# Storing the last 64 rows of each batch two batches at a time, and adding the last item in two halves

## The chip, the core and the metric

The kernel runs on one core of one Trainium2 chip. The metric is the device time of one execution in microseconds. The three runs of the kernel before the change took 427.37, 427.93 and 429.17 us; their median, 427.93 us, is the time before.

## What is computed

Eight batches of eight heads of sparse attention (576 positions, head width 64) are followed by a spectral mixing layer and a residual layer. With `x` the attention output of shape (8, 576, 512):

```python
X = np.fft.rfft(x, axis=1)
Y[:, :n_modes] = Yr + 1j * Yi        # 64 modes, each with its own complex 512x512 matrix w_r, w_i
y = np.fft.irfft(Y, n=S, axis=1)
u = x + y
return u + np.maximum(u @ w_ch, 0.0)
```

The output is 8 x 576 x 512 in float32, 9.44 MB. A batch is 576 rows of 512 floats, 2 KB a row.

## The kernel before

**Up to the last stage.** The kernel computes strided and local attention, takes the Fourier coefficients of the result, and multiplies the 64 modes by their matrices while those are fetched. The matrices are fetched by `w_fetch` through the GpSimd queue, with conversion to half precision. A usual fetch (L186) has 64 partitions with two rows of 2048 numbers each. Three pairs of modes, named in `UNEVEN`, have the first of their two fetches cut into pieces (L182): of 25, 12 and 27 partitions, of 6, 54 and 4, and of 10 and 54.

**The last stage, from about 395 us.** The residual `u` and the product `u @ w_ch` are finished and stored item by item. The list `items` has 18 entries. The first 16 are a pair of batches and one of four blocks `t` of 128 rows of each. The last two, with `t == 4`, are the rows 512 to 575, of batches 0 to 3 (item 16) and of batches 4 to 7 (item 17, `LAST`). An item fills a tile `osb` of 128 partitions x 2 x 512 floats, 512 KB. For `t < 4` each of the two halves `osb[:, j]` is one batch. For `t == 4` the half `osb[:, i]` holds two batches: the first in partitions 0 to 63, the second in partitions 64 to 127.

**Steps of one item.** TensorE adds the inverse transform to two sums that are held in PSUM (`v_early`, `u_early`, `new_rows`). `v_done` (L1013) applies Relu on ScalarE. `u_done` (L1020) adds the two sums on VectorE into `osb` and issues the stores. The function `pieces` says in how many slices `v_done` and `u_done` work: two for item 0, one for all others.

**Stores.** For `t < 4` an item is stored from SyncE (L1028): one transfer with 128 partitions outermost and two rows of 2 KB in each, or, for item 0, two transfers of 256 KB. For `t == 4` the kernel before issues one transfer of 128 KB for each batch (L1031), even batches from SyncE and odd ones from ScalarE; each has 64 rows of 2 KB on both sides.

**Order.** The program order is the order on each engine. In round `k` of the last loop `v_done(k)` stands before `u_done(k - 1)`, so ScalarE applies the Relu of item 17 before it issues the stores of item 16. Nothing of the kernel follows `u_done(17)` but the end of the program (L1108 in the trace), which waits for the stores. `osb` shares its five buffers with the fetched matrices; no fetch is left in the last stage.

Of the kernel before, what the change touches and what calls it, by code (L numbers as in the profile page):

```python
# [56 lines left out]
def kernel(  # L57
# [10 lines left out]
    nc = tc.nc  # L68
# [169 lines left out]
    def normalise(val, den, n, pieces, dst):  # L238
        rec = pin.tile([128, 8], FP, tag="rec", bufs=4, name="rec")
        nc.vector.reciprocal(out=rec[0:n, 0:pieces], in_=den)  # L240
        nc.vector.tensor_tensor(  # L241
            out=dst,
            in0=val.rearrange("p h (q c) -> p h c q", c=4),
            in1=rec[0:n, 0:pieces]
            .to_broadcast((n, pieces, 64))
            .rearrange("p h (q c) -> p h c q", c=4),
            op=AluOp.mult,
        )
# [718 lines left out]
    for n, i in enumerate([3, 5, 7] + list(range(8, 21))):  # L967
        b, t = n // 2, n % 2 * 2
# [8 lines left out]
    LAST = len(items) - 1  # L977
# [25 lines left out]
            )  # L1003

    def pieces(k):
        return [slice(0, 1), slice(1, 2)] if k == 0 else [slice(0, 2)]

    def v_done(k):
        rl = ptr.tile([128, 2, 576], FP, tag=("xT", "rl")[k // 2 % 2], bufs=2, name="rl")
        rls[k] = rl[:, :, 0:DM]  # L1010
        vp = vps.pop(k)
        for j in pieces(k):
            nc.scalar.activation(out=rls[k][:, j], in_=vp[:, j], func=ACTF.Relu)  # L1013

    def u_done(k):
        bs, t = items[k]
        up, rl = ups.pop(k), rls.pop(k)
        osb = pw.tile([128, 2, DM], FP, tag="w", name="osb")
        for j in pieces(k):
            nc.vector.tensor_tensor(  # L1020
                out=osb[:, j], in0=up[:, j], in1=rl[:, j], op=AluOp.add
            )
            if t < 4:
                rows = out[:, ds(128 * (t - t % 2), 256), :].rearrange(
                    "b (p i) e -> p b i e", i=2
                )
                own_b = slice(bs[0] + j.start, bs[0] + j.stop)
                nc.sync.dma_start(rows[:, own_b, t % 2], osb[:, j])  # L1028
        if t == 4:
            for b in bs:  # L1030
                (nc.scalar if b % 2 else nc.sync).dma_start(  # L1031
                    out[b, ds(512, 64), :], osb[ds(64 * (b % 2), 64), b // 2 % 2, :]
                )

    flush()
# [24 lines left out]
    for k in range(2):  # L1060
        if k:
            u_early(k)
        new_rows(k, ups[k], yys)
        u_done(k)
    for k in range(2, LAST + 2):
        if k == 8:
            held = psum("p", pair=True)[:, 0]
            spec_z(3, 1, held)
            act_copy(zzs[1], held)
        if k <= LAST:  # L1070
            v_early(k)
        if k > 2:
            u_early(k - 1)
        if k <= LAST:
            new_rows(k, vps[k], zzs)
        if k > 2:
            new_rows(k - 1, ups[k - 1], yys)
        if k <= LAST:
            v_done(k)
        if k > 2:  # L1080
            u_done(k - 1)
# [31 lines left out]
```

## Time and profile before

| what | value |
|---|---|
| runs | 427.37, 427.93, 429.17 us; median 427.93 us |
| profiled execution | the page gives its span, 426.7 us, 1.2 us under the median of the runs |
| busy share of the span | PE 81%, VectorE 55%, ScalarE 51%, GpSimd 26% |
| output stores | 17 from L1028, 8 from L1031 |
| first store issued, last store issued | 396.88 us, 422.32 us |
| last store landed | 425.58 us |
| granted TensorE clock, mean | 0.926 |

Times are counted from the first instruction of the profiled execution. In the answers on the trace, a line of a timeline has its start, its duration, the engine, the source line, the operation, the output and input tiles, and in brackets the idle time before it and what ended it; `SPq` and `ACTq` are the instruction queues of SyncE and ScalarE, where stores are issued. In a table by stretches there stand the busy time of each engine with its instructions in brackets, then the granted clock, the mean busy share of the 16 DMA engines, and the rate in GB/s. In the list of DMA issues stand the tiles, the queue, the count, the size of each, and the median time in us from issue to landing.

### The profile page before, as it was taken

What the parts mean: (1) busy time and instruction counts of PE and PEld (TensorE: products, weight loads), DVE (VectorE), ACT (ScalarE), POOL (GpSimd) and SP (SyncE); (2) the same over time, 40 slices, a digit from 0 to 9 for tenths busy, and PEclk for the clock granted to TensorE, in tenths of its full rate; (3) what the DMA queues carried; (4) which work ended last, traced back from release to release, by engine and by line L of the source; (5) the groups of instructions that cost most, each with busy time, mean ns of one, the idle gap of its engine ahead of it and who ended that gap; (6) DMA issues with size and microseconds to landing.
All of it is one profiled execution on the core that took longest, in us unless ns stands there. A gap on an engine that the chain in (4) does not pass through costs nothing.

```text
span 426.7 us, 9768 instructions
## 1 busy us (share of the span) xinstructions
PE 346.4 (81%) x4167; PEld 208.2 (49%) x4167; DVE 234.7 (55%) x466; ACT 218.3 (51%) x390; POOL 110.7 (26%) x196
## 2 busy tenths in 40 slices
PE   2977878769999698889768788878788867889993
PEld 2866767554656365566433344435444423445330
DVE  3788778851355154356113246746676354655884
ACT  1687678643656356556642235423442444443872
POOL 8332333322423222222222322222232222210000
PEclk9999899967999689999995889989999979989997
DMA  8999999999999999999999999999999999995698
GB/s 150 210 212 212 213 213 213 211 211 211 214 213 213 213 213 215 212 214 215 210 214 211 213 214 213 210 213 215 212 213 214 213 213 214 214 212 105 244 355 287
DMA packets 30938, 91.62 MB, mean 215 GB/s; under 512 B 4464, under 2 KB 5232, under 8 KB 30896
## 3 DMA queue, kind: packets, MB, share of 16 engines
q0 software_dynamic: 25168, 81.28, 96.2%
q1 hardware_dynamic: 4976, 9.13, 5.9%
q10 hardware_dynamic: 752, 0.61, 0.5%
q8 instruction: 32, 0.52, 0.5%
q14 instruction: 10, 0.08, 0.0%
HBM read 162.83 MB, written 9.44 MB: 404 GB/s over the span
## 4 chain that ended last, share of the span: by engine, by line
DMA 47%; PE 29%; DVE 14%; ACT 5%; issue 3%; DVEq 0%; POOL 0%; ACTq 0%; POOLq 0%
DMA wt<-in_moe_w_i_dram 38%; DMA wt<-in_moe_w_r_dram 7%; PE y L597 5%; DVE xb L241 3%; DVE kz L283 3%; PE p L987 2%; ACT X L251 2%; PE sc L532 2%; PE tp L413 2%; PE sc L459 1%; PE p L1001 1%; PE y L532 1%; PE p L760 1%; DVE yy L752 1%; DVE rec L240 1%
## 5 line engine op out<-in xcount | busy, mean ns | idle before, releaser
L597 PE MATMUL y<-wt,X 128*32 128x512 f16 (+1 forms) x448 | 70.9, 430 | 20.1 <-DMA wt<-in_moe_w_i_dram 20.1
L186 POOL DMA_DIRECT2D wt<-in_moe_w_r_dram x59 | 34.7, 588 | 126.4 <-PE y L597 56.3
L186 POOL DMA_DIRECT2D wt<-in_moe_w_i_dram x60 | 35.4, 590 | 68.3 <-DMA wt<-in_moe_w_i_dram 44.4
L597 PEld LDWEIGHTS <-X 128*32 128x32 f16 (+1 forms) x448 | 28.1, 140 | 39.4 <-DMA wt<-in_moe_w_i_dram 18.6
L727 DVE COPY xo<-tp 128x512 f16<-128x512 f16 x32 | 22.1, 691 | 36.8 <-PE tp L725 36.8
L726 ACT ACTIVATE v<-sc 128x512 f16<-128x512 f32 x32 | 19.1, 597 | 44.2 <-PE sc L717 44.2
L717 PE MATMUL sc<-w_cp,xT 128*128 128x512 f16 x128 | 36.9, 410 | 1.9 <-DVE xT L690 1.9
L489 ACT ACTIVATE PL<-sc 128x480 f16<-128x480 f32 (+1 forms) x48 | 27.0, 578 | 21.3 <-PE sc L475 21.0
L241 DVE TENSOR_TENSOR xb<-av,rec 90x256 f16<-90x256 f32 (+2 forms) x80 | 36.0, 450 | 2.8
L240 DVE RECIPROCAL rec<-av 90x4 f32<-90x4 f32 (+2 forms) x80 | 14.6, 183 | 39.3 <-PE av L504 28.2
L251 ACT ACTIVATE yr<-y 128x512 f16<-128x512 f32 x28 | 16.7, 597 | 36.8 <-PE y L597 35.6
L961 DVE TENSOR_TENSOR xo<-p,xo 128x1024 f16<-128x1024 f32 x16 | 19.6, 1225 | 21.7 <-PE p L760 21.7
L420 DVE COPY qT<-tp 128x576 f16<-128x576 f16 x16 | 11.9, 752 | 34.7 <-PE tp L413 34.7
L251 ACT ACTIVATE v<-p 128x1024 f16<-128x1024 f32 x16 | 16.4, 1023 | 23.1 <-PE p L760 23.1
L378 ACT ACTIVATE PL<-sc 90x360 f16<-90x360 f32 (+1 forms) x48 | 22.7, 490 | 7.0 <-PE sc L371 6.4
L251 ACT ACTIVATE v<-tp 128x640 f16<-128x640 f16 (+1 forms) x24 | 19.0, 807 | 11.8 <-PE tp L447 9.3
L413 PE MATMUL tp<-cI_s,ring 64*64 64x64 f16 x864 | 22.4, 197 | 2.7 <-DVE qT L420 2.4
L459 PE MATMUL sc<-cMl_s,cI_s 128*128 128x480 f16 (+1 forms) x48 | 19.4, 405 | 4.5 <-ACT PL L489 2.9
L276 PE MATMUL tp<-cI_s,ring 72*128 72x72 f16 x256 | 15.4, 207 | 8.7 <-DMA ring<-in_v_dram 7.1
L413 PEld LDWEIGHTS <-ring 64*64 64x64 f16 x864 | 17.5, 110 | 9.4 <-issue 5.4
L251 ACT ACTIVATE kz<-tp 64x360 f16<-64x360 f16 (+1 forms) x32 | 18.9, 592 | 6.2 <-PE tp L413 5.2
L1013 ACT ACTIVATE rl<-p 128x1024 f32<-128x1024 f32 (+1 forms) x19 | 18.4, 979 | 5.7 <-PE p L1001 3.1
(142 smaller groups left out, 737.9 us busy)
## 6 DMA issues: line engine op xcount, KB each, us to landing
wt<-in_moe_w_i_dram POOLq DMA_DIRECT2D x60, 512.0 KB, 18.8
wt<-in_moe_w_r_dram POOLq DMA_DIRECT2D x59, 512.0 KB, 17.7
out_dram<-osb SPq DMA_DIRECT2D x15, 512.0 KB, 3.4
ring<-in_v_dram POOLq DMA_DIRECT2D x8, 288.0 KB, 13.4
ring<-in_q_dram POOLq DMA_DIRECT2D x8, 288.0 KB, 13.6
ring<-in_k_dram POOLq DMA_DIRECT2D x8, 288.0 KB, 13.1
ring<-in_v_dram POOLq DMA_DIRECT2D x3, 512.0 KB, 14.8
ring<-in_q_dram POOLq DMA_DIRECT2D x3, 512.0 KB, 14.8
```

What stands on the lines that cost most here:

```text
L186: nc.gpsimd.dma_start(dst, rows)
L241: nc.vector.tensor_tensor(out=dst, in0=val.rearrange("p h (q c) -> p h c q", c=4), in1=rec[0:n, 0:pieces] .to_broadcast((n, pieces, 64)) . ...
L251: nc.scalar.activation(out=out, in_=in_, func=ACTF.Copy)
L378: nc.scalar.activation(out=PS[0:n, ds(POFF[t], 4 * n)], in_=scp[0:n, 0 : 4 * n], func=ACTF.Exp, scale=SCALE,)
L413: nc.tensor.transpose(tp[ds(64 * hp, 64), ds(64 * i, 64)], qn[ds(64 * hp, 64), ds(64 * (9 * g + i), 64)], idn[ds(64 * hp, 64), ds(64 * hp, ...
L459: nc.tensor.matmul(scp[:, 0 : n * times].rearrange("p (h x) -> p h x", h=times), idn, mask_rows("cMl", n, times), start=True, stop=False,)
L489: nc.scalar.activation(out=dst, in_=src, func=ACTF.Exp, scale=SCALE)
L597: nc.tensor.matmul(yp[ds(a, 32), :], Xh[half][pr, c].rearrange("p b r (h m) -> p (b r h) m", h=2)[:, :, mm % 32], wt[pr, XC[c], :], start= ...
L717: nc.tensor.matmul(vp, xT[:, ch], w_chs["cp"][:, ch, :], start=(ch == 0), stop=(ch == 3),)
L726: nc.scalar.activation(out=v0, in_=vp, func=ACTF.Copy)
L727: nc.vector.tensor_copy(out=xo.rearrange("p (h q c) -> p h q c", h=2, c=4), in_=tp[:, 0:512].rearrange("p (h c q) -> p h q c", h=2, c=4),)
L961: nc.vector.tensor_tensor(out=xo, in0=up[:, 0:n], in1=xo, op=AluOp.add)
```

## The change

`pieces` gives two slices for the last item as well, so its Relu and its sum are each done in two instructions of 128 x 512 instead of one of 128 x 1024. The stores of the items 16 and 17 are issued in the loop over the slices, one transfer for each half of `osb` instead of one for each batch: source `osb[:, i]`, 128 partitions of 2 KB; destination two batches, 64 rows of 2 KB in each. The half 0 is stored from SyncE and the half 1 from ScalarE. For item 16, which has one slice, both are issued after its sum; for item 17 each is issued after its own half of the sum.

```diff
     def pieces(k):
-        return [slice(0, 1), slice(1, 2)] if k == 0 else [slice(0, 2)]
+        return [slice(0, 1), slice(1, 2)] if k in (0, LAST) else [slice(0, 2)]
...
                 nc.sync.dma_start(rows[:, own_b, t % 2], osb[:, j])
-        if t == 4:
-            for b in bs:
-                (nc.scalar if b % 2 else nc.sync).dma_start(
-                    out[b, ds(512, 64), :], osb[ds(64 * (b % 2), 64), b // 2 % 2, :]
+                continue
+            for i in range(2)[j]:
+                (nc.scalar if i else nc.sync).dma_start(
+                    out[ds(bs[2 * i], 2), ds(512, 64), :], osb[:, i]
                 )
```

## The prediction

> **What bounds the kernel now.** The change touches nothing before the last two of 18 items, so I read the page only for the span and then went to the end of the trace: the table by stretches, the list of store issues, the timeline of the last items. First the span, and the table by stretches; its last two columns are the busy share of the DMA engines and GB/s.
>
> ```profile
> span 426.7 us, 9768 instructions
> ```
> ```profile
> 410.00:418.00 8.00, 8.00 (x51) 2.56 (x50) 7.28 (x7) 6.33 (x7) 0.00 (x0) 1.00 1.01 376
> 420.00:421.00 1.00, 0.00 (x0) 0.00 (x0) 1.00 (x2) 0.00 (x0) 0.00 (x0) 1.00 1.03 393
> 421.00:422.00 1.00, 0.00 (x0) 0.00 (x0) 0.28 (x1) 0.00 (x0) 0.00 (x0) 0.96 0.94 244
> 422.00:425.00 3.00, 0.00 (x0) 0.00 (x0) 0.00 (x0) 0.00 (x0) 0.00 (x0) 0.50 0.88 307
> 425.00:426.70 1.70, 0.00 (x0) 0.00 (x0) 0.00 (x0) 0.00 (x0) 0.00 (x0) 0.50 0.00 0
> ```
>
> From 410 us on, all 16 DMA engines are full with stores; TensorE is full too until 418, but from 421.3 us no engine computes, and the DMA engines work on until 425. So the end is set by the stores: the last packet ends at 425.05 us by the trace's packet records, the last landing is at 425.58 (0.53 later), the span ends 1.1 after that. Whatever the stores of items 16 and 17 gain or lose arrives in the time in full.
>
> The timeline of the last two sums and the eight stores that the change replaces, and the list of store issues:
>
> ```profile
> 418.92 1.23 DVE L1020 TENSOR_TENSOR osb<-p,rl 128x1024 f32<-128x1024 f32 x1 [0.31 <-PE p L1001]
> 420.06 1.22 DVE L1020 TENSOR_TENSOR osb<-u,rl 128x1024 f32<-128x1024 f32 x1
> 420.17 2.44 SPq L1031 DMA_DIRECT2D out_dram<-osb  x4
> 420.18 2.75 ACTq L1031 DMA_DIRECT2D out_dram<-osb  x4
> ```
> ```profile
> out_dram<-osb SPq DMA_DIRECT2D x15, 512.0 KB, 3.4
> out_dram<-osb SPq DMA_DIRECT2D x2, 256.0 KB, 2.4
> out_dram<-osb SPq DMA_DIRECT2D x4, 128.0 KB, 2.8
> out_dram<-osb ACTq DMA_DIRECT2D x4, 128.0 KB, 3.3
> ```
>
> Four issues on each queue take 2.4 to 2.8 us, and the last goes out at 422.32, 1.0 us after the last sum ended. Every store is cut into packets of one row, 2 KB; a packet takes one DMA engine 84 to 85 ns (median), both at 397.5 us with one small store in flight and at 424.5 us with most engines idle. That is a price of the engine, not of the crowd.
>
> **What a transfer's outermost count does.** All 25 stores have 128 or 64 rows outermost, and each raises its semaphore at sixteen separate times, one for each DMA engine. The new destination has 2 batches outermost (64 rows inside), against 128 partitions in the source. No transfer of the SyncE and ScalarE queues in this trace has an outermost count under 64, so I looked for such transfers elsewhere, and found the cut fetches of L182 on the GpSimd queue. Issue times, then time to landing:
>
> ```profile
> 254.24 0.59 POOL L186 DMA_DIRECT2D wt<-in_moe_w_i_dram  x1 [1.62 <-DMA wt<-in_moe_w_i_dram]
> 257.07 0.59 POOL L182 DMA_DIRECT2D wt<-in_moe_w_r_dram  x1 [2.24 <-PE tp L685]
> 259.18 0.71 POOL L182 DMA_DIRECT2D wt<-in_moe_w_r_dram  x1 [1.52 <-DMA wt<-in_moe_w_i_dram]
> 261.62 0.61 POOL L182 DMA_DIRECT2D wt<-in_moe_w_r_dram  x1 [1.73 <-DMA wt<-in_moe_w_r_dram]
> ```
> ```profile
> wt<-in_moe_w_i_dram POOLq DMA_DIRECT2D x1, 512.0 KB, 19.5
> ...
> wt<-in_moe_w_r_dram POOLq DMA_DIRECT2D x1, 48.0 KB, 16.9
> ...
> wt<-in_moe_w_r_dram POOLq DMA_DIRECT2D x1, 432.0 KB, 19.0
> ...
> wt<-in_moe_w_r_dram POOLq DMA_DIRECT2D x1, 32.0 KB, 16.9
> ```
>
> The whole fetch of 64 partitions lands at 254.24 + 19.5 = 273.7 us; its three successors, of 6, 54 and 4 partitions and 512 KB in sum, at 274.0, 278.2 and 278.5: 4.8 us for what whole fetches land in 2.46 us. Between the first and the last of the sixteen semaphore marks of one fetch, whole fetches keep their distance for dozens in a row (6.1 to 6.4 us here); the fetch of 54 raises it from 6.28 to 9.90, and the one of 54 at 299.97 us brings it back from 9.11 to 5.58. A whole fetch is 128 packets, 8 for each engine, so a packet costs 2.46/8 = 0.307 us there. 3.6 us is 12 packets: 54 partitions x 2 rows = 108 packets lie on nine engines (12 each), and the other seven get none. Nine is the largest divisor of 54 that is not over 16. So on this queue the work is dealt out by the outermost count, in equal shares, and a count with no divisor near 16 leaves engines idle. For an outermost count of 2 that is two engines, 64 packets each.
>
> [...]
>
> **Part by part.** *Relu in halves:* two instructions of 0.594 us (the 128x512 rows of L1013) for one of 1.02, +0.17 us on ScalarE. The Relu of item 17 starts at 418.65 and would end at 419.84; VectorE is busy with item 16 until 420.15, which hides it; without that cover it costs 0.17. *Sum in halves:* two of 0.686 us for one of 1.22; from 420.06 the halves end at 420.75 and 421.43 instead of 421.28, +0.15 us for the second, −0.53 for the first. *Issues:* four instead of eight; SyncE at 420.17 and about 420.8, ScalarE at 420.18 and about 421.5 (the last 0.8 us earlier than now). ScalarE's stores stand behind the Relu of item 17, as before; behind them stands only the end of the program, on both queues. *Where the waiting goes:* to the DMA engines.
>
> *The new transfers.* They are 4 x 128 = 512 packets of 2 KB. The unknown is the number n of engines that share them. Its ends are 16 (the nearest stores, by size and source) and 2 (the nearest outermost count, by the rule the cut fetches show). I take 2: the two transfers differ from the stores of 256 KB at 397 us in nothing but the outermost count, and that is what the fetches react to. An engine's packet period in the full stretch is 16 x 2048 B / 377 GB/s = 87 ns. The engines come free of the store issued at 418.64 (landed 421.58 to 421.87, less the 0.53) at about 421.3. Then
>
> - n = 2: 512/2 = 256 packets x 0.087 = 22.3 us, last packet at 443.6, landing 444.1, span 445.2: +18.5 us.
>
> The second item's transfers queue behind the first's, which alone last 11 us, so their issue time costs nothing. The period has its own ends: 81 ns, the shortest packets (20.7 us, +17.0), and 94 ns, from 422 to 425 with both queues on an engine (16 x 0.88 x 2048 / 307; 24.1 us, +20.4). From 421.5 to 422.0 the packets, then almost all of one 64-partition half, took 162 ns in the median; two engines on different halves shouldn't meet that, and I keep it out of the range (41.5 us, +38).
>
> The median of the runs is 427.93, so I forecast 427.93 + 18.5 = 446.4 us. Against the 426.7 of the span this is the same 18.5.
>
> **The rivals.** *All 16 engines.* The destination's batches are dealt row by row. For it: nothing on these two queues shows another number than sixteen. Against it: the fetch of 54. Price: after 420.0 us the table has 393 + 244 + 334 + 326 + 260 (the stretch from 422 to 425 in single microseconds) = 1557 KB; at 380 GB/s, without the slow 64-row packets, they take 4.1 us and end at 424.1 instead of 425.05. That is at best −0.95, 427.0 us; if only the halves' delay shows, +0.15, 428.1. Either is within 0.5%, which is 2.1 us and about what a measurement of this kernel can tell from no change. The tail ends at 421.3 + 512 x 0.087/n, which meets the present 425.05 at n = 12: with 12 engines or more the change is not slower, at 8 it costs 1.8 us, so this rival decides the sign.
>
> *Two pairs of engines.* SyncE's and ScalarE's transfers go to different pairs: n = 4, 11.1 us, last packet at 432.4, +7.4, 435.3 us. For it: the trace doesn't say which engines a small count gets, and the distance between the first and last mark went up after one fetch of 54 and down after another, so there it was not always the same nine. Against it: that is the GpSimd queue; all sixteen engines serve SyncE's and ScalarE's stores alike now, and nothing in the trace keeps the two queues apart.
>
> **How the numbers follow.** Two engines 0.85, two pairs 0.04, sixteen 0.11. The likeliest case gives 446.4. Its range goes from +17.0 less the 0.6 by which the fastest run lies under the median and a microsecond for an earlier start (443.3), to +20.4 with the 1.2 by which the slowest lies over it and two for pauses between the queues (451.5); I leave a twentieth of the case outside, so it holds 0.81 and need not reach to the others. Slower by over 0.5%: 0.85 + 0.04 = 0.89; of the sixteen-engine case 0.10 within 0.5%, and 0.01 for a gain over 2.1 us, which no term here supplies.
>
> **What would show it.** Right: four stores at L1031 with 256 KB; DMA share near 0.125 and about 47 GB/s (2 x 2048/0.087) from 422 to 443; landings 11 us after the issue for item 16 and over 20 us for item 17; sums ending at about 420.75 and 421.4. Wrong: landings within 3.5 us and a span that ends near 426 (sixteen engines); 94 GB/s and 432 (two pairs); some 25 GB/s would be two engines with packets of 160 ns.

## The result: 446.36 us, 4.3% slower

The changed kernel takes 446.36 us in the median of four runs (445.82 to 446.80), against 427.90 us of the kernel before, the median of four runs (the three given above and one of 427.87 us). The ratio is 1.0429, with a 95% interval from 1.0416 to 1.0442. The profiled execution took 445.82 us; its span is 444.0 us, against 426.7.

**The profile after.** First the table by stretches of the changed kernel. Its last two columns are the busy share of the 16 DMA engines and the rate in GB/s.

```profile
410.00:418.00 8.00, 8.00 (x55) 2.41 (x52) 7.04 (x7) 6.01 (x7) 0.00 (x0) 1.00 1.02 377
...
420.00:421.00 1.00, 0.00 (x0) 0.00 (x0) 0.34 (x1) 0.00 (x0) 0.00 (x0) 1.00 0.40 127
421.00:422.00 1.00, 0.00 (x0) 0.00 (x0) 0.00 (x0) 0.00 (x0) 0.00 (x0) 1.00 0.12 20
...
425.00:432.00 7.00, 0.00 (x0) 0.00 (x0) 0.00 (x0) 0.00 (x0) 0.00 (x0) 0.50 0.13 51
432.00:440.00 8.00, 0.00 (x0) 0.00 (x0) 0.00 (x0) 0.00 (x0) 0.00 (x0) 0.50 0.13 51
...
442.00:444.00 2.00, 0.00 (x0) 0.00 (x0) 0.00 (x0) 0.00 (x0) 0.00 (x0) 0.50 0.02 9
```

Up to 418 us nothing has changed: the DMA engines are full, at 377 GB/s. From 421 to 442 us the share is 0.12 to 0.13, which is two engines of sixteen (0.125). They move 20 GB/s at first and 51 GB/s from 425 us. No engine computes in that time.

Then the timeline of the last two sums and of the four stores, and the list of store issues:

```profile
417.92 1.22 DVE L1020 TENSOR_TENSOR osb<-p,rl 128x1024 f32<-128x1024 f32 x1 [0.31 <-PE p L1001]
...
419.07 1.28 DVE L1020 TENSOR_TENSOR osb<-u,rl 128x512 f32<-128x512 f32 x2
419.18 1.30 SPq L1031 DMA_DIRECT2D out_dram<-osb  x2
419.18 2.00 ACTq L1031 DMA_DIRECT2D out_dram<-osb  x2
```
```profile
out_dram<-osb SPq DMA_DIRECT2D x15, 512.0 KB, 3.5
...
out_dram<-osb ACTq DMA_DIRECT2D x2, 256.0 KB
```

All of the last stage lies about 1.0 us earlier in this execution (the last sum starts at 419.07 us, not 420.06); the instructions are the same up to there. The two halves of the last sum take 1.28 us together, against 1.22 for one. The list gives no time to landing for the ScalarE stores of 256 KB, where every store before had one. It looks for sixteen semaphore marks, and these have three. From the trace's records, in us:

```
store            issued    first mark   later marks
item 16, SyncE   419.18    420.41       430.90  431.05
item 16, ScalarE 419.18    420.88       433.94  433.95
item 17, SyncE   419.95    420.88       441.16  441.31
item 17, ScalarE 420.65    421.60       442.67  442.75
```

One mark comes 0.9 to 1.7 us after the issue (that of item 16's ScalarE store at 420.88 us, while ScalarE's first packet of 2 KB starts at 423.3), and then one for each of two engines. The same records show that both queues share one pair of engines. These packets are consecutive ones, each of 2 KB and each recorded with 84 ns:

```
start us   queue
424.001    SyncE      424.002    SyncE
424.081    ScalarE    424.082    ScalarE
424.161    SyncE      424.162    SyncE
424.241    ScalarE    424.242    ScalarE
```

Every 80 ns two packets start, in turn from the one queue and the other. Two pairs of engines would start four in that time.

### The profile page after: what moved, and what is told of

It is laid out like the page before. It is cut to its first block, busy times and chain, and to the rows that moved or that the text cites. A ratio compares the mean times of both kernels' runs of the same rounds, so it can differ in the third digit from the quotient of the medians.

```text
span 444.0 us, 9766 instructions
## 1 busy us (share of the span) xinstructions
PE 340.1 (77%) x4167; PEld 205.6 (46%) x4167; DVE 234.9 (53%) x467; ACT 218.2 (49%) x391; POOL 111.1 (25%) x196
## 4 chain that ended last, share of the span: by engine, by line
DMA 49%; PE 16%; DVE 5%; ACT 2%; issue 2%; POOL 0%; DVEq 0%; ACTq 0%; POOLq 0%
DMA wt<-in_moe_w_i_dram 35%; DMA wt<-in_moe_w_r_dram 11%; PE y L597 4%; DMA ring<-in_k_dram 4%; PE p L987 2%; PE p L1001 1%; DVE yy L752 1%; PE sc L717 1%; ACT X L251 1%; PE tp L413 1%; PE y L532 1%; PE sc L459 1%; PE p L992 1%; DVE xb L241 1%; PE u L992 1%
## 5 line engine op out<-in xcount | busy, mean ns | idle before, releaser
L597 PE MATMUL y<-wt,X 128*32 128x512 f16 (+1 forms) x448 | 67.4, 410 | 23.4 <-DMA wt<-in_moe_w_i_dram 22.7
L727 DVE COPY xo<-tp 128x512 f16<-128x512 f16 x32 | 22.1, 692 | 38.8 <-PE tp L725 38.7
L420 DVE COPY qT<-tp 128x576 f16<-128x576 f16 x16 | 11.9, 752 | 32.1 <-PE tp L413 32.1
L413 PE MATMUL tp<-cI_s,ring 64*64 64x64 f16 x864 | 22.3, 196 | 3.0 <-DVE qT L420 2.7
## 6 DMA issues: line engine op xcount, KB each, us to landing
ring<-in_v_dram POOLq DMA_DIRECT2D x3, 512.0 KB, 14.8
ring<-in_q_dram POOLq DMA_DIRECT2D x3, 512.0 KB, 14.8
```

Source lines behind the costliest of these rows:

```text
L413: nc.tensor.transpose(tp[ds(64 * hp, 64), ds(64 * i, 64)], qn[ds(64 * hp, 64), ds(64 * (9 * g + i), 64)], idn[ds(64 * hp, 64), ds(64 * hp, ...
L597: nc.tensor.matmul(yp[ds(a, 32), :], Xh[half][pr, c].rearrange("p b r (h m) -> p (b r h) m", h=2)[:, :, mm % 32], wt[pr, XC[c], :], start= ...
L727: nc.vector.tensor_copy(out=xo.rearrange("p (h q c) -> p h q c", h=2, c=4), in_=tp[:, 0:512].rearrange("p (h c q) -> p h q c", h=2, c=4),)
```

## The experiments

The theory is that a transfer is dealt out to a number of DMA engines that divides its outermost count, so that the new stores have two engines. The rivals say that the store's form (two batches in one transfer), the work in halves, or a row-by-row dealing decides. The diffs are against the changed kernel in the first, second and ninth run, and against the kernel before in the others. All ratios are to the kernel before, which was run beside each group of runs and had medians of 427.73 to 427.99 us there. They stand with their 95% interval and need not equal the quotient of two medians.

**Each part of the change alone: the transfers.**

```diff
-        return [slice(0, 1), slice(1, 2)] if k in (0, LAST) else [slice(0, 2)]
+        return [slice(0, 1), slice(1, 2)] if k == 0 else [slice(0, 2)]
```

> The four transfers of 256 KB with two batches outermost, without the split of item 17: its Relu and sum are one instruction each again, and both its stores are issued after the whole sum. Theory (the transfers are dealt to two DMA engines by the outermost count of 2, and everything else is small): the second item's packets queue behind 128 packets of the first on each of the two engines anyway, so their later issue costs nothing: 446.4 us, within 0.4 of the changed kernel. Rival (a part of the 18.5 us comes from working the last item in halves): less than 446 by that part.

Measured: 445.95 us, ratio 1.0422 (1.0409 to 1.0436). The transfers alone carry the loss; the interval overlaps that of the whole change.

**The halves alone.**

```diff
-            for i in range(2)[j]:
-                (nc.scalar if i else nc.sync).dma_start(
-                    out[ds(bs[2 * i], 2), ds(512, 64), :], osb[:, i]
+            for b in bs[2 * j.start : 2 * j.stop]:
+                (nc.scalar if b % 2 else nc.sync).dma_start(
+                    out[b, ds(512, 64), :], osb[ds(64 * (b % 2), 64), b // 2 % 2, :]
```

> Item 17 in two halves, its four stores of 128 KB, one for each batch, issued after the half that they belong to; item 16 and all transfers as before. Theory: the second half of the sum ends 0.15 us later, the first 0.5 us earlier, and the queues still need about 0.57 us for each of eight issues, so the last issue stays near 422.3: 427.5 to 428.2 us, no difference. Rival (the halves carry part of the loss): clearly over 429.

Measured: 428.03 us, ratio 1.0007 (0.9998 to 1.0016): no difference. In its trace SyncE's last issue starts 1.9 us and ScalarE's 2.2 us after the first, as in the kernel before; the eight issues follow one another closely, and the earlier half of the sum does not draw them forward.

**Two batches in one transfer, but 64 rows outermost.** This keeps the size, the number of transfers and the two batches in each, and changes which count is outermost; the two batches are now those that share 64 partitions.

```diff
-            for b in bs:
-                (nc.scalar if b % 2 else nc.sync).dma_start(
-                    out[b, ds(512, 64), :], osb[ds(64 * (b % 2), 64), b // 2 % 2, :]
+            for i in range(2):
+                (nc.scalar if i else nc.sync).dma_start(
+                    out[bs[i] : bs[i] + 3 : 2, ds(512, 64), :].rearrange(
+                        "b p e -> p b e"
+                    ),
+                    osb[ds(64 * i, 64)],
```

> Again two transfers of 256 KB and two batches for each of the items 16 and 17, but those two batches that lie in the same 64 partitions (0 and 2, 1 and 3, and so on), so that both sides have 64 rows outermost and the two batches inside; no halves. Theory (the outermost count deals the work): 64 gives sixteen engines; four issues instead of eight, the last at about 421.4 instead of 422.3: 427.0 to 428.0 us. Rival (a destination in two batches, or transfers of 256 KB at this place, is slow by itself): about 446.

Measured: 428.54 us, ratio 1.0013 (1.0003 to 1.0023). The 18 us are gone, so two batches in one transfer are not what costs. But the run is no faster than the kernel before, though its last store was issued at 421.10 us, 1.25 us after the start of its last sum; in the kernel before it was 2.26. The gain is lost again in a slow stretch, which its table shows:

```profile
421.00:422.00 1.00, 0.00 (x0) 0.00 (x0) 0.06 (x1) 0.00 (x0) 0.00 (x0) 1.00 0.85 199
422.00:423.00 1.00, 0.00 (x0) 0.00 (x0) 0.00 (x0) 0.00 (x0) 0.00 (x0) 1.00 0.93 207
...
424.00:425.00 1.00, 0.00 (x0) 0.00 (x0) 0.00 (x0) 0.00 (x0) 0.00 (x0) 0.51 0.96 352
```

The engines count as busy, but move 199 and 207 GB/s: from 421.5 to 422.5 a packet takes 160 to 172 ns (medians of half a microsecond), and 84 ns again after that. The kernel before has such a stretch too, but a shorter one: 244 GB/s from 421 to 422, and 334 in the microsecond after it.

**The same for item 16, with item 17 in halves.**

```diff
-        return [slice(0, 1), slice(1, 2)] if k == 0 else [slice(0, 2)]
+        return [slice(0, 1), slice(1, 2)] if k in (0, LAST) else [slice(0, 2)]
...
-        if t == 4:
-            for b in bs:
-                (nc.scalar if b % 2 else nc.sync).dma_start(
-                    out[b, ds(512, 64), :], osb[ds(64 * (b % 2), 64), b // 2 % 2, :]
+                continue
+            for i in range(2):
+                pr = ds(64 * i, 64)
+                (nc.scalar if i else nc.sync).dma_start(
...
+                        if k < LAST
+                        else (out[bs[2 * j.start + i], ds(512, 64), :], osb[pr, j.start])
```

> Item 16 stored as in the run with 64 rows outermost, two transfers of 256 KB; item 17 in two halves, each stored by two transfers of 128 KB after its own half of the sum. Theory: sixteen engines throughout; six issues, those of the first half 0.5 us before the whole sum would have ended: 426.9 to 428.0 us. If the issue of the stores is what ends last in the kernel before, this and the run with 64 rows outermost come out up to 0.9 us under it; if the bytes alone do, they come out equal to it.

Measured: 428.67 us, ratio 1.0009 (1.0001 to 1.0018). Neither earlier data nor fewer issues brings anything. That fits an end that is set by the bytes and not by the issues, but does not show it alone, since the slow stretch stands in this run too (159 to 167 ns from 421.5 to 422.5) and can hide a small gain.

**The count alone: 60, 62 and 61 rows.** Three kernels that differ from the kernel before in one number, one batch in each store, as before.

```diff
-                    out[b, ds(512, 64), :], osb[ds(64 * (b % 2), 64), b // 2 % 2, :]
+                    out[b, ds(512, 60), :], osb[ds(64 * (b % 2), 60), b // 2 % 2, :]
```

> The kernel before, with each of the last eight stores cut to its first 60 rows of 64 (four rows of each batch are not stored). Theory (a transfer runs on the largest number of engines up to sixteen that divides its outermost count): 60 gives fifteen engines with 4 packets for each store, as now: 427.4 to 428.2 us. Rival (the count is dealt row by row over all engines): the same.

> The kernel before, with each of the last eight stores cut to its first 62 rows of 64 (two rows of each batch are not stored). Theory: 62 has only 2 as a divisor up to sixteen, so two engines with 31 packets for each of eight stores, 248 in all; at the 0.080 us from packet to packet that the changed kernel shows, 19.8 us from about 421.3, and 1.6 more to the end: span about 442.8, time about 444 us, though each store has one batch and fewer bytes than before. Rival (two batches in one transfer are what costs, or rows are dealt over all engines): 427.4 to 428.2 us.

> The kernel before, with each of the last eight stores cut to its first 61 rows of 64 (three rows of each batch are not stored). Theory: 61 is prime, so one engine takes all 488 packets: 39 us at 0.080 us each, span about 462, time about 463 us. Rival (rows are dealt over all engines): 427.4 to 428.2 us.

Measured: 60 rows 427.40 us, ratio 0.9994 (0.9984 to 1.0003); 62 rows 446.01 us, 1.0430 (1.0415 to 1.0446); 61 rows 465.38 us, 1.0886 (1.0870 to 1.0902). The stretches of 62 rows, then of 61 rows:

```profile
432.00:440.00 8.00, 0.00 (x0) 0.00 (x0) 0.00 (x0) 0.00 (x0) 0.00 (x0) 0.50 0.13 51
```
```profile
432.00:440.00 8.00, 0.00 (x0) 0.00 (x0) 0.00 (x0) 0.00 (x0) 0.00 (x0) 0.50 0.07 26
```

Two engines of sixteen, and one (0.0625). A store's marks are one at the start and then 15 with 60 rows, 2 with 62 and 1 with 61. Row-by-row dealing is refuted on these queues: from 61 rows, one more takes 19 us off the time and one less 38. Both slow runs came out 2.0 and 2.4 us over the figure that was expected; that is taken up below.

**Item 16 alone by the new transfers.**

```diff
-            for b in bs:
+            for i in range(2) if k < LAST else ():
+                (nc.scalar if i else nc.sync).dma_start(
+                    out[ds(bs[2 * i], 2), ds(512, 64), :], osb[:, i]
+                )
+            for b in bs if k == LAST else ():
```

> Item 16 alone by the two transfers of 256 KB with two batches outermost; item 17 as before, four stores of 128 KB, no halves. Theory: two engines get 128 packets for item 16 and then 16 for item 17 behind them in their queues, 144 in all, 11.5 us at 0.080 us each from about 421.3: span about 434.4, time about 435.6 us. Rival (item 17's stores are the end of the kernel, and a slow store of the item before is hidden behind them): about 428 us.

Measured: 436.81 us, ratio 1.0223 (1.0206 to 1.0241), about half the loss. The stores of item 17 have sixteen engines but don't hide those of item 16: two of their sixteen shares stand behind item 16's packets. From its table by stretches:

```profile
425.00:432.00 7.00, 0.00 (x0) 0.00 (x0) 0.00 (x0) 0.00 (x0) 0.00 (x0) 0.50 0.21 63
```

The share starts higher, while the other engines finish item 17, and comes to a mean of 0.21. Item 17's first store, issued at 420.49 us, got fourteen of its sixteen marks by 424.83 and the last two at 431.07 and 431.28, 10.8 us after its issue.

**All four new transfers from one queue.**

```diff
-                (nc.scalar if i else nc.sync).dma_start(
+                nc.sync.dma_start(
```

> The changed kernel with all four transfers of 256 KB issued from SyncE instead of two from each queue. Theory: the two queues meet on the same two engines, so the 256 packets of each engine only come in another order: 20.5 us at 0.080 us, and the time stays near 446.4. The changed kernel also lost about 1.6 us at the start (30 packets between 420.4 and 423 us where two engines move some 62): if that comes from two queues preparing their packets at once, one queue gets it back, 444.7 us; if not, 446.4. Rival (two pairs of engines, one for each queue): one queue then has one pair, 20 us; two had 10: the time would rise by 10, which the changed kernel's 80 ns already speak against.

Measured: 445.88 us, ratio 1.0413 (1.0399 to 1.0426). One queue or two, 51 GB/s either way:

```profile
421.00:422.00 1.00, 0.00 (x0) 0.00 (x0) 0.00 (x0) 0.00 (x0) 0.00 (x0) 1.00 0.10 20
...
424.00:432.00 8.00, 0.00 (x0) 0.00 (x0) 0.00 (x0) 0.00 (x0) 0.00 (x0) 0.50 0.13 51
```

Two pairs of engines are refuted. The slow start (20 GB/s from 421 to 422) is there with one queue as well, so it does not come from two queues preparing packets at once.

**The 64-row transfers from one queue.** The edit is that of the third run with `nc.sync` for both transfers.

> The kernel of the run with 64 rows outermost (two batches inside, 256 KB), with all four transfers issued from SyncE. That run gained nothing, and its packets took 160 ns from 421 to 422.5 us, while only transfers out of partitions 0 to 63 moved, and 84 ns when both queues had moved on. Theory (a transfer out of one 64-partition half, alone, moves at half the rate): with one queue each of the four transfers is alone, 512 packets on 16 engines at 0.16 us, 5.1 us from about 421.3, last packet at 426.4 against 425.05 in the kernel before: 429.0 to 429.8 us. Rival (the slow packets belong to the start of a queue): 427.7 to 428.7 us.

Measured: 428.57 us, ratio 1.0015 (1.0006 to 1.0023). My theory of the half rate fell: with one transfer after the other the kernel is not slower than with two queues. Its stretches:

```profile
421.00:422.00 1.00, 0.00 (x0) 0.00 (x0) 0.00 (x0) 0.00 (x0) 0.00 (x0) 0.85 0.95 193
422.00:425.00 3.00, 0.00 (x0) 0.00 (x0) 0.00 (x0) 0.00 (x0) 0.00 (x0) 0.50 0.88 281
```

Of the 512 packets of its last four stores, the first 128 took 157 to 168 ns (medians of 64), and the other 384 took 84 to 86, though they come from one 64-partition half after the other just the same. In this run the slow packets belong to the start of these stores; the next run shows that this is not the whole of it, and the cause stays open.

**The 64-row items moved forward,** so that an item of 128 rows comes last and is stored in two halves of 128 partitions.

```diff
-    items += [(range(b, b + 4), 4) for b in (0, 4)]
+        items.insert(4 + 9 * P0 // 2, (range(2 * P0, 2 * P0 + 4), 4))
...
-        return [slice(0, 1), slice(1, 2)] if k == 0 else [slice(0, 2)]
+        return [slice(0, 1), slice(1, 2)] if k in (0, LAST) else [slice(0, 2)]
...
-                (nc.scalar if b % 2 else nc.sync).dma_start(
+                nc.sync.dma_start(
...
-        if k == 8:
+        if k == 9:
```

> The kernel before with the two items of the last rows put earlier among the 18 (as the fifth and the fourteenth), their eight stores of 128 KB all issued from SyncE, and the last item, now of 128 rows in each of two batches, worked and stored in two halves of 256 KB like the first item. All transfers have 64 or 128 outermost. Theory: the last sum ends at about 421.4, its second store of 128 partitions lands 2.4 us later, at 423.9, or when the bytes are through, at 424.6; span 425.7 to 426.2: 426.8 to 427.6 us. If the slow packets of one 64-partition half only move to the middle of the stage, where the DMA engines are full as well, 427.6 to 428.4 us: no difference.

Measured: 428.43 us, ratio 1.0011 (1.0002 to 1.0020). It came out at the upper edge of the second reading, as its stretches show:

```profile
418.00:420.00 2.00, 1.49 (x10) 0.39 (x8) 1.93 (x3) 1.42 (x3) 0.00 (x0) 1.00 0.87 254
...
422.00:425.00 3.00, 0.00 (x0) 0.00 (x0) 0.00 (x0) 0.00 (x0) 0.00 (x0) 0.89 1.03 387
```

The end now runs at 387 GB/s, but a slow stretch stands at 418 to 420, where the engines would have been full as well (386 GB/s there in the kernel before). Another stands at the first of the two items that were moved. Its four stores were issued one every 0.6 us from 402.85, and from 404.0 to 406.5 all of them ran slowly: 155 ns in the median of their 256 packets. So slow packets are not only those at the start of the stage's 64-row stores. A half rate for each 64-partition half would explain this item, but not the 384 fast packets of the run before; no run here separates the causes. No version that stores all rows beats the kernel before.

## Why the prediction was right

**The step that carried it** was the number of engines, read from fetches of another queue. The count runs show that number on SyncE's and ScalarE's queues: 15, 2 and 1 engines for 60, 62 and 61 rows, the largest divisor up to sixteen, and 2 for 128 partitions against two batches. That all four transfers share the same two engines, as the sum's 256 packets for each engine have it, no trace of the kernel before shows; the alternating packets of the changed kernel showed it, and the run with one queue gave the same 51 GB/s.

**The working of 18.5 us** came out at 18.46 in the medians, but that it agrees so closely is luck: two errors cancel. The packet period was 80 ns, not 87: 256 packets take 20.5 us and not 22.3. Against that, the start was slow: the two engines were free at about 420.2 us, but moved only 30 packets from 420.5 to 423.0, where their full rate is some 62. No step of mine had that; the slow packets that I had seen in the kernel before, I took to come from one 64-partition half alone and left out. From their release to the last packet (442.42) it was 22.2 us, against 22.3 forecast, so the slow start took about 1.7 us. From there to the end of the span it was 1.6 us, as forecast (0.33 to the last landing and 1.28 more, against 0.53 and 1.1). The upper end of the range has a slip: 24.1 us less 22.3 gives +20.3, not +20.4. The profiled span alone would give +17.3, because that execution had reached the last stage 1.0 us earlier.

The signs that I had named were there, with two sizes off: 51 GB/s for 47, and for item 16 landings after 11.9 us on SyncE but 14.8 on ScalarE, where I had said 11 for both: the two queues take turns, and the first packet of ScalarE's came only at 423.3 us. Item 17's stores landed after 21.4 and 22.1 us.

Three of the experiments' expectations took the 80 ns but not the slow start, and so were low: by 2.0 us with 62 rows, by 2.4 with 61 and by 1.2 with item 16 alone.

**The small terms** stayed small. In the trace the Relu in halves took 1.08 us against 1.02, and the sum 1.28 against 1.22: 0.06 us more each, not 0.17 and 0.15. In the time, working in halves showed no cost and no gain (0.9998 to 1.0016). That the second item's issue time costs nothing was right: without the halves, with a later issue, the loss was the same.

**The rivals.** Two pairs of engines fell with the alternating packets and with the one-queue run. Sixteen engines never came about with two batches outermost; made to come about, by 64 rows outermost, it gave 428.54, past the 427.0 to 428.1 that I had priced for it. What failed in that price is the tail at 380 GB/s "without the slow 64-row packets": in the three runs with that form the packets were slow for more than a microsecond at the start.

## What to carry to other kernels

Before merging transfers, look at the outermost count of both sides: here the kernel took 446.36, 446.01 and 465.38 us with 2, 62 and 61 outermost, against 427.90 with 64, whether the store was larger or smaller, because it ran on two engines or one. Read it from the DMA share (0.13 and 0.07 here), from the semaphore marks of one transfer, or, before any change, from a transfer of the same trace whose count is no multiple of 16. The transfers on two engines also held up what was queued behind them there, even where that had all sixteen: with item 16 alone by the new transfers, a store of 128 KB landed 10.8 us after its issue, against a median of 2.8 for such stores in the kernel before.

## What the runs showed that was not expected

- The first packets of the last stores were slow wherever their form differs from the 128-partition stores before them: some 160 ns for 2 KB with 64 rows outermost, 200 ns and more with 60, up to 425 ns in the changed kernel, up to 846 ns with 62 rows, for half a microsecond (60 rows) to nearly three (the changed kernel). The item stored with 128 partitions at the end of the last run did not have it; the item of 64 rows that was moved forward in that run had it in 224 of its 256 packets (over 120 ns). The cause is open.
- An issue took longer where much lay on few engines. SyncE's four issues took 0.30, 0.45, 6.7 and 10.0 us with 61 rows on one engine, and ScalarE's last took 4.6 us with 62 rows on two; with 60 rows all took 0.3 to 0.7 us. With all four new transfers from SyncE, the third and fourth issue took 3.6 and 4.7 us. Nothing of the kernel stood behind them here.
- A packet of 2 KB started every 80 ns on an engine, whether one engine ran (26 GB/s), or two (51 GB/s); sixteen full ones gave 377 to 393 GB/s, a period of 83 to 87 ns.
